# ReLU-squared attention and a gated MLP on one core: queries split earlier, weights decoded earlier, TensorE fed zeros at the start, casts ahead of halves

## The chip, the cores and the metric

One core of a Trainium2 chip runs the whole program. The metric is the time on the device of one execution, in microseconds (us). The engines of the core work side by side, each through its own instructions in order: TensorE (PE: matmuls, with the weight loads PEld beside them), VectorE (DVE), ScalarE (ACT), GpSimd (POOL), and SyncE (SP), which here issues every DMA. TensorE reads from the on-chip memory SBUF and writes only to the accumulators in PSUM, of which the kernel uses eight tiles of 128 x 512 floats.

## The reference

```python
# u, v: (4, 3008, 256)   z: (4, 3008, 64)   w_gate, w_val: (256, 1536)   w_out: (1536, 256)
scores = (1.0 / S) * np.matmul(z, z.transpose(0, 2, 1))
attn = np.maximum(scores, 0.0) ** 2
x = (u * np.matmul(attn, v)).reshape(B * S, D)
rms = np.sqrt(np.mean(x * x, axis=-1, keepdims=True) + 1e-06)
xn = x / rms * rms_g
g = xn @ w_gate
silu = g * (1.0 / (1.0 + np.exp(-g)))
out = (silu * (xn @ w_val) @ w_out).astype(np.float32)
```

Inputs arrive as float32 (z, u, v) and, for the weights, as 64-bit floats, which the kernel takes apart into 32-bit words itself.

## The kernel before

**Precision.** TensorE multiplies in a short float format (float32r). Every operand is therefore split into a high half (a cast) and a low half (operand minus high half), and a product is three matmuls: high by high, low by high, high by low. Keys have 64 dimensions only, so their high and low half stand in the two halves of the 128 partitions, and a score product is two matmuls. The cast is mostly ScalarE's work and the subtraction VectorE's; for the batches after the first, and for the weights, GpSimd does subtractions in pieces of 128 columns (L133, L348).

**Tiling.** A batch of 3008 rows is cut into six column groups of at most 512 queries, two to a pair, so there are 12 pairs, three in a batch. For each pair p there are two phases. Phase ("A", p) is the attention: 24 steps, one for each tile of 128 keys, the last tile having 64. Phase ("M", p) is the norm and the MLP: 12 units, one for each 128 columns of the hidden layer, with three slots each, so slots 0 to 35. The MLP's two input products are done as one 2 x 2 block product with seven products in place of eight (Winograd's form); A11, A12, S1, S2, S3, A22, S4 name the seven operands of x, in the order in which a unit takes them. The order of phases is A0, A1, A2, M0, A3, M1, A4, M2 and so on: the attention runs three pairs ahead.

**A step of an attention phase** (`phase_a`). Step i issues the score product of step i+2 (`emit_s`: high and low half of the queries, tiles mh0, ml0, mh1, ml1, against a key tile in zst; ScalarE's ReLU; VectorE's multiplication ReLU times score, L416), then the halves of step i+1 (`emit_l`: H by ScalarE's cast, L438, and L by VectorE's subtraction, L441), then the jobs hooked on step i, then the product of step i with v (`emit_av`, L482, L483, L487: six matmuls for each of two column groups). For the tile of 64 keys the low half is put into the other 64 partitions of H (L445), and the product is four matmuls. In some steps (`is_square`) ScalarE makes the square itself, twice (L435, L436), and VectorE's multiplication drops out. Scores are symmetric: from the second batch on, a tile whose mirror image will be needed later is also copied as two 16-bit halves (`halves`, L456 on VectorE or L458 on ScalarE) and stored; the mirror is later loaded transposed (`load_turned`), and its score product is left out. In the first batch this happens only within the third pair.

**At the end of a pair** the products with v of the last two steps are put off in a queue (`pend`): the second half of step 22, and the two halves of step 23, each of which is followed by its gate (L512: accumulator times u, read by VectorE, then stored). Between them, `enter_a` issues the next pair's first two score products. The next pair's queries are loaded into buffers of tag `raw` and split by VectorE (L290 high, L291 low, `prep_mov`) at step 22.

**Around the phases.** During the first three attention phases, which have 72 steps counted through, the weights are decoded: a part is a load, one square on ScalarE, five VectorE operations (L154, L160, L166, L170, L174) and sums on GpSimd; then the seven combinations of each of three groups of weights are made, split and stored to DRAM (L133, L224, L229), and in each MoE unit loaded again (wu). The norm of a pair (squares, sums, a root by a cubic and two Newton steps in small operations L563 to L584, scaling) and the split of its x (L642 high, L647 low) are hooked on steps of a later attention phase or are placed by a planner (`Beside`) on slots of an MLP phase: it gives VectorE 0.75 us of room in each slot and ScalarE 1.35 in each third one, and puts each job in the first slot with room. The planner also places the next batch's key and value casts (`plan_batch`), each a given number of slots after its load.

**The start** loads the first keys and v, splits them and begins; the first pair's queries come from the same load as the first keys.

Of the kernel before, what the change touches and what calls it, by code (L numbers as in the profile page):

```python
# [19 lines left out]
P = 128  # L20
CH = 512
# [9 lines left out]
def kernel(  # L31
# [84 lines left out]
    def prep_const():  # L116
        nc.vector.memset(warm, 0.0)

        nc.scalar.activation(warm, warm, AF.Silu)
        nc.sync.dma_start(out=g_sb, in_=gT)  # L120
        nc.sync.dma_start(out=fold_sb, in_=fold)
# [152 lines left out]
    def prep_mov(p, k):  # L274
# [12 lines left out]
        def split():  # L287
            mh = moving.tile([P, CH], F32R, tag=f"mh{k}", name="mh")
            ml = moving.tile([P, CH], F32R, tag=f"ml{k}", name="ml")
            nc.vector.tensor_scalar(mh[:, :n], tiles["raw"][:, :n], SCALE, None, op0=ALU.mult)  # L290
# [5 lines left out]
        return load, split, tiles  # L296
# [87 lines left out]
    def is_square(p, i, k):  # L384
        return p < LAG and (i + k) % 2 == 1 and not is_turned(p, i, k) and (p < LAG - 1 or i < NK - 8)
# [40 lines left out]
    def emit_l(p, i, ks=(0, 1)):  # L426
        b, c0 = where(p)[:2]
        kt = order(p)[i]
        for k in ks:
# [16 lines left out]
            att[p, i, k] = (hi, lo)  # L446
            kc = kt // 4
            if kc > c and keeps(b, c, kc):
# [6 lines left out]
                if c0 == 0 and copies[0] % 5 in (1, 3):  # L455
# [454 lines left out]
    def plan_splits(p, phase, slots):  # L910
        jobs_ = split_jobs_at(p)
        if p == 0:
            jobs_ = [jobs_[i] for i in (2, 3, 6, 5, 4, 0, 1)]
# [9 lines left out]
    def plan_batch(b):  # L923
# [4 lines left out]
        for k, (load, one, two) in enumerate(todo):  # L928
            if k == NC and b == 1:
                m.put(norm_plan(1)[:13], 3)  # L930
# [5 lines left out]
            h = m.put([("a", 0.6, 0, one), ("d", 0.7 if dve else 0.0, 0, two)], s + 2)  # L936
# [17 lines left out]
    plan_splits(0, ("A", 2), [16, 17, 18, 19, 20, 21, 22])  # L954
    at(("A", 2), NK - 1, lambda: load_x(1))
    for p in range(1, NPAIR):
# [6 lines left out]
        if p == 1:  # L963
            for i, (e, cost, gap, fn) in enumerate(norm_plan(1)[13:]):
# [20 lines left out]
    for p in range(1, NPAIR):  # L985

        for k in range(2):
            load, split, _ = prep_mov(p, k)
# [4 lines left out]
            else:  # L993
                at(("A", p - 1), NK - (5 if p == 1 else 10), load)
                at(("A", p - 1), NK - 2, split)
# [32 lines left out]
    for j, steps, end in ((0, (5, 9, 13, 17), 26), (1, (24, 28, 32, 36), 39), (2, (40, 44, 48, 51), 54)):  # L1028
# [6 lines left out]
    for f, g in zip(range(0, 8, 2), (54, 58, 62, 66)):  # L1035
        plan_part(prep_wout(f), g)

    with tc.manual_schedule():
# [6 lines left out]
        for c in range(2):  # L1045
            first["z", c][1]()
            first["m", c][1]()
            first["z", c][2]()
            if c == 0:
                first["v", 0][1]()  # L1050
                first["v", 0][2]()
        emit_s(0, 0)
        first["v", 1][1]()
        emit_s(0, 1)
        first["v", 1][2]()
        emit_l(0, 0)
        for p in range(LAG):
            phase_a(p)
            if p + 1 < LAG:
                for go in enter_a(p + 1):  # L1060
                    go()
                    pend.popleft()()
# [46 lines left out]
```

## Time and profile before

| | |
|---|---|
| median of 3 runs | 2063.69 us (2063.58 to 2065.18) |
| the profiled execution | 2068.19 us, span 2066.4 us |
| TensorE busy | 2028.0 us, 98% of the span, 8968 matmuls |
| VectorE busy | 1598.0 us, 77% |
| ScalarE busy | 1448.5 us, 70% |
| GpSimd busy | 217.3 us, 11% |
| DMA | 320.50 MB, 155 GB/s |

The span runs from the first to the last instruction of the profile. A busy time is the union of an engine's instructions; a matmul's own duration (387 to 389 ns on the mean) overlaps with the next, so one comes about every 0.22 us. The releaser of a wait is the instruction that ended it. PEclk is the clock granted to TensorE as a share of 2.4 GHz.

### The profile page before, as it was taken

What the parts mean: (1) busy time and instruction counts of PE and PEld (TensorE: products, weight loads), DVE (VectorE), ACT (ScalarE), POOL (GpSimd) and SP (SyncE); (2) the same over time, 40 slices, a digit from 0 to 9 for tenths busy, and PEclk for the clock granted to TensorE, in tenths of its full rate; (3) what the DMA queues carried; (4) which work ended last, traced back from release to release, by engine and by line L of the source; (5) the groups of instructions that cost most, each with busy time, mean ns of one, the idle gap of its engine ahead of it and who ended that gap; (6) DMA issues with size and microseconds to landing.
All of it is one profiled execution on the core that took longest, in us unless ns stands there. A gap on an engine that the chain in (4) does not pass through costs nothing.

```text
span 2066.4 us, 27204 instructions
## 1 busy us (share of the span) xinstructions
PE 2028.0 (98%) x8968; PEld 1679.2 (81%) x8968; DVE 1598.0 (77%) x2633; ACT 1448.5 (70%) x2601; POOL 217.3 (11%) x376
## 2 busy tenths in 40 slices
PE   8998999999999999999999999999999999999999
PEld 7787778788888888888887888788888788888887
DVE  7788988997867778787775876878777677777765
ACT  8887867785686666697577675679657757466665
POOL 0155845100000000400000000220000000000000
PEclk9999999999999999999999999999999999999999
DMA  3245375254555496337365458634545637734342
GB/s 109 67 129 166 104 251 191 89 189 169 138 153 191 125 211 203 130 142 226 114 165 168 148 140 196 218 110 164 197 128 132 210 134 159 198 119 161 124 145 91
DMA packets 320654, 320.50 MB, mean 155 GB/s; under 512 B 196736, under 2 KB 235776, under 8 KB 320512
## 3 DMA queue, kind: packets, MB, share of 16 engines
q1 hardware_dynamic: 320512, 318.77, 50.8%
q8 instruction: 70, 1.15, 0.2%
q14 instruction: 72, 0.59, 0.1%
HBM read 190.78 MB, written 81.79 MB: 132 GB/s over the span
## 4 chain that ended last, share of the span: by engine, by line
PE 76%; DVE 2%; ACT 2%; DMA 1%; issue 1%; SPq 0%; ACTq 0%; DVEq 0%
PE ps L681 10%; PE ps L682 9%; PE ps L683 9%; PE po L482 9%; PE po L483 9%; PE po L487 8%; PE py L709 5%; PE py L713 5%; PE py L710 5%; PE ps L402 3%; PE ps L401 3%; DMA raw<-in_zT 1%; ACT s L688 1%; ACT hH L693 1%; DMA out_T<-y 0%
## 5 line engine op out<-in xcount | busy, mean ns | idle before, releaser
L482 PE MATMUL po<-H,vh 128*128 128x512 f32 (+1 forms) x1152 | 448.7, 389 | 7.7 <-DVE H L445 5.1
L483 PE MATMUL po<-H,vl 128*128 128x512 f32 (+1 forms) x1152 | 445.8, 387 | 0.0
L688 ACT COPY s<-ps 128x512 f32<-128x512 f32 (+1 forms) x432 | 250.0, 579 | 221.8 <-PE ps L683 221.8
L681 PE MATMUL ps<-xh,wu 128*128 128x512 f32 (+1 forms) x1008 | 392.4, 389 | 7.4 <-ACT s L688 4.9
L683 PE MATMUL ps<-xl,wu 128*128 128x512 f32 (+1 forms) x1008 | 389.1, 386 | 2.9 <-DVE xl L647 2.9
L682 PE MATMUL ps<-xh,wu 128*128 128x512 f32 (+1 forms) x1008 | 389.2, 386 | 0.4 <-DMA wu<-wc 0.2
L487 PE MATMUL po<-L,vh 128*128 128x512 f32 (+1 forms) x1104 | 337.9, 387 | 4.4 <-DVE L L441 4.2
L693 ACT CAST hH<-s 128x512 fp32r<-128x512 f32 (+1 forms) x288 | 177.0, 615 | 200.3 <-DVE s L775 197.1
L441 DVE TENSOR_TENSOR L<-r,H 128x512 fp32r<-128x512 f32 x368 | 254.7, 705 | 50.7 <-ACT H L438 29.0
L416 DVE TENSOR_TENSOR r<-ps,r 128x512 f32<-128x512 f32 x328 | 214.4, 680 | 98.3 <-ACT r L409 97.7
L409 ACT ACTIVATE r<-ps 128x512 f32<-128x512 f32 (+1 forms) x392 | 215.7, 597 | 105.8 <-PE ps L402 95.1
L698 DVE TENSOR_TENSOR hL<-s,hH 128x512 fp32r<-128x512 f32 (+1 forms) x288 | 199.6, 693 | 107.4 <-ACT hH L693 94.2
L482 PEld LDWEIGHTS po<-H,vh 128*128 128x128 f32 x1152 | 216.8, 188 | 58.3 <-DVE H L445 11.2
L483 PEld LDWEIGHTS po<-H,vl 128*128 128x128 f32 x1152 | 217.1, 188 | 40.1
L487 PEld LDWEIGHTS po<-L,vh 128*128 128x128 f32 x1104 | 206.9, 188 | 48.1 <-DVE L L441 9.5
L681 PEld LDWEIGHTS ps<-xh,wu 128*128 128x128 f32 x1008 | 189.3, 188 | 53.0 <-ACT s L688 12.9
L709 PE MATMUL py<-hH,woh 128*128 128x512 f32 (+1 forms) x576 | 222.5, 386 | 0.1
L710 PE MATMUL py<-hH,wol 128*128 128x512 f32 (+1 forms) x576 | 222.1, 386 | 0.0
L683 PEld LDWEIGHTS ps<-xl,wu 128*128 128x128 f32 x1008 | 189.3, 188 | 39.6 <-DVE xl L647 3.6
L682 PEld LDWEIGHTS ps<-xh,wu 128*128 128x128 f32 x1008 | 189.4, 188 | 35.7 <-DMA wu<-wc 1.2
L438 ACT CAST H<-r 128x512 fp32r<-128x512 f32 x328 | 202.2, 626 | 1.9 <-DVE r L416 1.9
L348 POOL TENSOR_TENSOR vl<-raw,vh 128x128 fp32r<-128x128 f32 x144 | 78.9, 584 | 981.8 <-ACT vh L337 981.8
(82 smaller groups left out, 2915.4 us busy)
## 6 DMA issues: line engine op xcount, KB each, us to landing
wu<-wc SPq DMA_DIRECT2D x288, 448.0 KB, 4.0
kept<-halves SPq DMA_DIRECT2D x168, 256.0 KB, 2.0
raw<-in_v SPq DMA_DIRECT2D x44, 256.0 KB, 4.1
u<-in_uT SPq DMA_DIRECT2D x40, 256.0 KB, 4.5
xg<-u SPq DMA_DIRECT2D x40, 256.0 KB, 2.1
raw<-in_zT SPq DMA_DIRECT2D x38, 256.0 KB, 4.5
ux<-xg SPq DMA_DIRECT2D x16, 512.0 KB, 4.8
out_T<-y SPq DMA_DIRECT2D x32, 256.0 KB, 2.2
```

What stands on the lines that cost most here:

```text
L409: nc.scalar.activation(a[:, :n], ps[:, :n], AF.Relu)
L416: nc.vector.tensor_tensor(a[:, :n], ps[:, :n], a[:, :n], op=ALU.mult)
L441: nc.vector.tensor_tensor(lo[:, :n], a[:, :n], f32(hi[:, :n]), op=ALU.subtract)
L482: nc.tensor.matmul(po[d][:, :n], wh[:, j, ds], hi[:, :n], start=(i == 0), stop=False)
L483: nc.tensor.matmul(po[d][:, :n], wl[:, j, ds], hi[:, :n], start=False, stop=(ends and lo is None))
L487: nc.tensor.matmul(po[d][:, :n], wh[:, j, ds], lo[:, :n], start=False, stop=ends)
L681: nc.tensor.matmul(ps[:, :n], wh[:, o, :], xh[:, :n], start=start, stop=False, skip_group_check=True)
L682: nc.tensor.matmul(ps[:, :n], wl[:, o, :], xh[:, :n], start=False, stop=False, skip_group_check=True)
L683: nc.tensor.matmul(ps[:, :n], wh[:, o, :], xl[:, :n], start=False, stop=stop, skip_group_check=True)
L688: nc.scalar.copy(s, ps[:, :self.n])
L709: nc.tensor.matmul(acc[h, d][:, :n], woh[:, f, ds], hi[:, :n], start=(f == 0), stop=False)
L710: nc.tensor.matmul(acc[h, d][:, :n], wol[:, f, ds], hi[:, :n], start=False, stop=False)
```

## The change

- `prep_const`: a tile of zeros (tag H, 512 columns) is written by VectorE, and TensorE multiplies it by itself eight times.
- The split of the queries gets two callable halves. At the start the order is: first keys' cast, query high, keys' low, query low, second query's split, v's cast, first score product; the second keys' cast and low half come after the first `emit_l`.
- `is_square`: for the first two pairs steps 22 and 23 are squared no more on ScalarE; for the third pair squares reach to step 21 instead of 15.
- `emit_l`: both casts and subtractions of a step come ahead of both copies into halves. The copies of the middle pairs of a batch (c0 = 2), too, go to VectorE two times in five.
- The x splits of the first pair run in the order of use, and one step earlier.
- `plan_batch`: eight instead of thirteen operations of the second pair's norm lie in M0; the others run in A3. The first two casts of a batch's keys start four slots after their loads, not two.
- Queries of the second and third pair: the first is split at step 21, the second at step 22.
- Decode parts, combinations and w_out parts begin earlier (of 72 steps): the parts at 4, 8, 12, 16, then 21, 25, 29, 33, then 37, 40, 43, 47; the combinations at 20, 36, 50; w_out at 50, 55, 59, 63.
- At a change of pair the put-off products go ahead of the next pair's score products, one for one.

```diff
+        idle = moving.tile([P, CH], F32R, tag="H", name="idle", bufs=5)
+        nc.vector.memset(f32(idle), 0.0)
+        none = ps_s.tile([P, CH], F32, tag="ps", name="ps")
+        for _ in range(8):
+            nc.tensor.matmul(none, idle[:, :P], idle, start=True, stop=True)
...
-        return p < LAG and (i + k) % 2 == 1 and not is_turned(p, i, k) and (p < LAG - 1 or i < NK - 8)
+        return p < LAG and (i + k) % 2 == 1 and not is_turned(p, i, k) and i < NK - 2
...
             att[p, i, k] = (hi, lo)
+            made_[k] = a
+        for k, a in made_.items():
+            c = c0 + k
+            n = width(c)
             kc = kt // 4
...
-                if c0 == 0 and copies[0] % 5 in (1, 3):
+                if c0 <= 2 and copies[0] % 5 in (1, 3):
...
-        if p == 0:
-            jobs_ = [jobs_[i] for i in (2, 3, 6, 5, 4, 0, 1)]
...
-                m.put(norm_plan(1)[:13], 3)
+                m.put(norm_plan(1)[:8], 3)
...
-            h = m.put([("a", 0.6, 0, one), ("d", 0.7 if dve else 0.0, 0, two)], s + 2)
+            h = m.put([("a", 0.6, 0, one), ("d", 0.7 if dve else 0.0, 0, two)], s + (4 if k < 2 else 2))
...
-    plan_splits(0, ("A", 2), [16, 17, 18, 19, 20, 21, 22])
+    plan_splits(0, ("A", 2), range(15, 15 + NO))
...
-            for i, (e, cost, gap, fn) in enumerate(norm_plan(1)[13:]):
+            for i, (e, cost, gap, fn) in enumerate(norm_plan(1)[8:]):
...
-                at(("A", p - 1), NK - 2, split)
+                at(("A", p - 1), NK - 3 + k, split)
...
-    for j, steps, end in ((0, (5, 9, 13, 17), 26), (1, (24, 28, 32, 36), 39), (2, (40, 44, 48, 51), 54)):
+    for j, steps, end in ((0, (4, 8, 12, 16), 20), (1, (21, 25, 29, 33), 36), (2, (37, 40, 43, 47), 50)):
...
-    for f, g in zip(range(0, 8, 2), (54, 58, 62, 66)):
+    for f, g in zip(range(0, 8, 2), (50, 55, 59, 63)):
...
-        for c in range(2):
-            first["z", c][1]()
-            first["m", c][1]()
-            first["z", c][2]()
-            if c == 0:
-                first["v", 0][1]()
-                first["v", 0][2]()
+        first["z", 0][1]()
+        first["m", 0][3]()
+        first["z", 0][2]()
+        first["m", 0][4]()
+        first["m", 1][1]()
+        first["v", 0][1]()
         emit_s(0, 0)
+        first["v", 0][2]()
         first["v", 1][1]()
         emit_s(0, 1)
+        emit_l(0, 0)
         first["v", 1][2]()
-        emit_l(0, 0)
+        first["z", 1][1]()
+        first["z", 1][2]()
...
                 for go in enter_a(p + 1):
+                    pend.popleft()()
                     go()
-                    pend.popleft()()
```

## Rows read from the trace of the kernel before

**Rows 1.** The page: busy us, share, instructions of each engine; engines' shares of the chain

```profile
PE 2028.0 (98%) x8968; PEld 1679.2 (81%) x8968; DVE 1598.0 (77%) x2633; ACT 1448.5 (70%) x2601; POOL 217.3 (11%) x376
...
PE 76%; DVE 2%; ACT 2%; DMA 1%; issue 1%; SPq 0%; ACTq 0%; DVEq 0%
```

**Rows 2.** TensorE's waits, whole span: total us, times, longest us

```profile
PE po L482 <- DVE H L445: 5.1, 7, 1.5
PE ps L681 <- ACT s L688: 4.9, 12, 1.9
...
PE po L487 <- DVE L L441: 4.2, 7, 1.0
PE ps L683 <- DVE xl L647: 2.9, 1, 2.9
PE ps L681 <- DVE s L775: 2.5, 1, 2.5
```

**Rows 3.** Windows: busy us (and count) by engine, granted clock, DMA share, GB/s

```profile
0.00:10.00 10.00, 4.30 (x10) 2.84 (x11) 4.97 (x9) 5.63 (x10) 0.20 (x4) 1.00 0.76 236
...
80.00:100.00 20.00, 18.37 (x72) 14.13 (x71) 13.73 (x23) 12.77 (x24) 4.50 (x8) 0.91 0.29 93
100.00:120.00 20.00, 18.89 (x83) 15.20 (x83) 15.50 (x26) 16.07 (x30) 3.69 (x8) 1.00 0.42 146
120.00:140.00 20.00, 20.00 (x90) 16.57 (x89) 17.90 (x28) 18.63 (x36) 12.46 (x20) 1.00 0.41 119
...
180.00:200.00 20.00, 15.55 (x55) 11.31 (x54) 14.40 (x23) 12.69 (x24) 13.58 (x24) 0.83 0.47 140
```

**Rows 4.** Windows by phase: third, first MoE block, first, second attention phase

```profile
198.00:280.50 82.50, 77.44 (x342) 63.24 (x343) 79.33 (x119) 68.39 (x130) 59.62 (x88) 1.00 0.50 147
280.50:380.00 99.50, 93.43 (x406) 75.05 (x404) 81.36 (x131) 66.36 (x122) 39.19 (x69) 1.00 0.58 192
10.50:92.00 81.50, 80.97 (x355) 66.29 (x354) 65.35 (x105) 72.30 (x134) 8.94 (x20) 1.00 0.21 65
93.00:184.50 91.50, 88.59 (x378) 71.50 (x378) 76.14 (x125) 76.17 (x141) 48.65 (x83) 0.98 0.42 127
```

**Rows 5.** Groups by line and shape: count, busy us, mean ns, idle before

```profile
L441 DVE TENSOR_TENSOR L<-r,H 128x512 fp32r<-128x512 f32 x340 | 235.2, 701 | 45.1 <-ACT H L438 26.0 <-ACT r L436 18.1
...
L458 ACT COPY halves<-r 128x1024 uint16<-128x1024 uint16 x126 | 134.6, 1068 | 5.5 <-DMA kept<-halves 4.1 <-DVE L L441 1.4
...
L456 DVE COPY halves<-r 128x1024 uint16<-128x1024 uint16 x42 | 28.8, 687 | 0.0
```

**Rows 6.** Timeline at the first change of pair: start, us, instruction, idle before

```profile
91.57 1.29 DVE L445 TENSOR_TENSOR H<-r,H 64x512 fp32r<-64x512 f32 x2 [0.49 <-ACT r L436]
...
93.37 0.49 PE L401 MATMUL ps<-mh,zst 128*128 128x512 f32 x1 [1.32 <-DVE mh L290]
...
103.14 0.47 PE L482 MATMUL po<-H,vh 128*128 128x512 f32 x1 [1.11 <-DVE u L512]
```

**Rows 7.** Timeline at the second change of pair

```profile
185.21 1.80 DVE L441 TENSOR_TENSOR L<-r,H 128x512 fp32r<-128x512 f32 x2
...
187.66 0.80 PE L401 MATMUL ps<-mh,zst 128*128 128x512 f32 x1 [3.34 <-DVE mh L290]
```

**Rows 8.** Timeline near the end of the first MoE block

```profile
369.37 0.38 DVE L584 SCALAR_TENSOR_TENSOR misc<-misc 128x32 f32<-128x32 f32 x1
```

**Rows 9.** Timeline in the MoE block of the seventh pair

```profile
1296.73 0.62 ACT L313 CAST zst<-raw 128x512 fp32r<-128x512 f32 x1 [3.88 <-DMA raw<-in_zT]
...
1298.40 0.50 PE L681 MATMUL ps<-xh,wu 128*128 128x512 f32 x1 [1.88 <-ACT s L688]
```

**Rows 10.** Window after that wait, TensorE alone: busy us (count), clock, DMA share, GB/s

```profile
1300.00:1320.00 20.00, 20.00 (x84) 0.93 0.62 203
```

**Rows 11.** Timeline at the fifth pair's tile of 64 keys

```profile
622.22 0.50 PE L482 MATMUL po<-H,vh 128*128 128x512 f32 x1 [0.77 <-DVE H L445]
```

**Rows 12.** Timeline at the second pair's tile of 64 keys

```profile
173.59 0.50 PE L482 MATMUL po<-H,vh 128*128 128x512 f32 x1 [0.93 <-DVE H L445]
```

More of the change, by code (lines that the diff above doesn't have):

```diff
@@ L285, in load, with high, low @@
             nc.sync.dma_start(out=raw[:, :n], in_=zT2[:, t0 + k * CH:t0 + k * CH + n])
-        def split():
-            mh = moving.tile([P, CH], F32R, tag=f"mh{k}", name="mh")
+        def high():
+            mh = tiles["mh"] = moving.tile([P, CH], F32R, tag=f"mh{k}", name="mh")
+            nc.vector.tensor_scalar(mh[:, :n], tiles["raw"][:, :n], SCALE, None, op0=ALU.mult)
+        def low():
+            mh = tiles["mh"]
             ml = moving.tile([P, CH], F32R, tag=f"ml{k}", name="ml")
-            nc.vector.tensor_scalar(mh[:, :n], tiles["raw"][:, :n], SCALE, None, op0=ALU.mult)
             nc.vector.scalar_tensor_tensor(
@@ L294, in split @@
             mov[p, k] = (mh, ml)
-        return load, split, tiles
+        def split():
+            high()
+            low()
+        return load, split, tiles, high, low
     def prep_stat(b, c, shared=None):
@@ L428, in emit_l @@
         kt = order(p)[i]
+        made_ = {}
         for k in ks:
@@ L987 @@
         for k in range(2):
-            load, split, _ = prep_mov(p, k)
+            load, split = prep_mov(p, k)[:2]
             if p >= LAG:
```

## The prediction, made before the change was run

> **What bounds the kernel now.** I read the page's busy shares and its chain first: the reader sees TensorE busy 98% of the span and holding 76% of the chain that ends last [rows 1]. No other engine can be the bound of the whole, so all a change of order can win is the time in which TensorE stands still or is clocked down. The profiled execution took 2068.19 us around a span of 2066.4; 2066.4 less 2028.0 busy is 38.4 us of standing still. The second view says on whom TensorE waits: the five rows of [rows 2] alone add up to 19.6 us. The third, the windows by time, says where. An undisturbed window has 90 matmuls in 20 us, 0.222 us each; the first 200 us hold the large holes [rows 3]. After that the losses are single waits, which the timeline places.
>
> I cut the losses into seven places, and price the change at each.
>
> **1. Start.** TensorE is busy 4.30 of the first 10 us, idle 5.70 until the first keys are split, and its first ten matmuls take 0.43 each [rows 3]. The change lets it multiply zeros meanwhile: one memset of 512 columns on VectorE, eight matmuls of about 0.43, 3.4 us in all, over before 5.7 if the memset ends before 2.2. It also puts the key's low half ahead of the query's, one operation of 0.7 (nearest row 0.701, [rows 5]) out of the way of the first product, and moves the second key cast and its subtraction behind the first weights. No row shows such a memset or the zeros; bounds: -0.5 us (the zeros run late and the keys wait) and +2.8 (0.7 plus ten matmuls at 0.222 instead of 0.43, 2.1). Since ScalarE and VectorE, not TensorE, feed the first products, I take the small end: 0.7.
> The row shows slow first matmuls after an idle start, although the granted clock reads 1.00 there [rows 3]. The Trainium skill (TensorE: Matmul & The Clock Gate, "Part 1: The HAM clock gate") says that the throttled state is the default and that activity releases it; by that rule the zeros would bring the full 2.1. Nothing below needs this.
>
> **2. First pair to second (80 to 104 us).** Lost now: 1.63 us idle and 0.09 of 20 us of clock, 1.8, in the first window, and 1.11 in the next, 4.5 in all [rows 3]. Before, both queries are split behind the last tile's two subtractions on VectorE (91.57 to 92.86), and TensorE, out of work, waits 1.32 us for the first (till 93.37) [rows 6]. After, the first query's two operations (0.5, from 92.86 to 93.37, and one like the 0.701 of [rows 5]; 1.2) go ahead of these, and one more six-matmul group (1.33 us) stands before the product. So the first query's half comes in time. The second query still queues behind the two subtractions, and VectorE carries more: two multiplications that ScalarE's squares did (2 x 0.701, 1.4), the first query's 1.2 and the first two operations of a decode part (at most 1.4; I take 1.0). Against this stand the idle shares: VectorE is busy 65.35 of 81.50 us in this phase [rows 4], 0.7 us free in a step of 16 matmuls (3.6 us), 2.1 over three steps. The subtractions then end near 92.86 + 1.4 + 1.2 + 1.0 - 2.1 = 94.4, the second query's halves at 94.9 and 95.6; TensorE arrives at 93.37 - 1.32 + 1.33 + 0.44 = 93.8. About 1.5 us of idle is left, as now. The gates (awaited 1.11 us until 103.14 [rows 6]) are split: the first column's comes early, the second's still stands behind four operations; I leave 0.8 of that wait. Half the clock loss may go, 0.9. Gain 0.1 + 0.3 + 0.9 = 1.3, between 0 and 4.5.
>
> **3. Second pair to third (180 to 200 us).** Lost now: 4.45 idle and 0.17 of 20 us of clock, 3.4: 7.85 [rows 3]. Here VectorE is late: its last two subtractions run 185.21 to 187.01, and TensorE waits 3.34 us until 187.66 [rows 7]. The same reordering gives 1.33 us of cover and takes the first query from behind them, but two multiplications (1.4) and the last operation of a part (0.7) come in ahead of the second query, and no idle time on VectorE is there to take them. Cover and price nearly cancel; I take 1.0 for a shorter slow stretch, between -1.5 and 7.
>
> **4. Third pair and its way into the MoE (198 to 285 us).** VectorE is busy 79.33 of 82.50 us [rows 4]: it is the bound of this phase, and TensorE's standing still is 5.06 us there. At its end TensorE waits 2.89 us for the low half of x [rows 2], since the splits of x were run in another order, the half needed first last. The change takes from VectorE here 1.4 decode parts (five operations each, 7 x 0.701 = 4.9 as an upper price; I take 4, as masks are shorter) and five multiplications (squares reach to step 21 instead of 15), 3.5: 7.5 us less. That is more than 5.06. It also runs the x splits one step earlier and in the order of use, so the 2.89 goes. ScalarE gains five passes like the cast of 0.62 in [rows 9], 3 us, and is busy 68.39 of 82.50, so it covers them, though not in steps 16 to 19 where I leave 1. And about 1.3 of the 5.06 is the wait for gates before 200 us, counted in place 3 (as the 1.11 of [rows 6], with a small second one). Gain 5.06 + 2.89 - 1 - 1.3 = 5.6; ends 1 and 7.9.
>
> **5. End of the first MoE block.** TensorE waits 2.5 us for VectorE [rows 2], which has just run the small operations of the norm's root, the last of them 0.38 us at 369.37 [rows 8]. Those thirteen move into the fourth pair's phase. The query split stays behind. What is late next is that split, 1.1 us for one query, which the slack of a MoE step took before. Two casts land in the block's last slot instead of one (0.6). Gain 2.4; ends 1 and 2.5.
>
> **6. Loads of the next batch's keys (MoE blocks of the fourth and seventh pair).** ScalarE, in order, stands 3.88 us at a cast for a load of z, and TensorE behind it 1.88 [rows 9]; the earlier twin is in the same row of [rows 2] (4.9 us, 12 times, most of the others 0.2). 4.9 - 1.88 - 10 x 0.2 leaves about 1.0 for it. The change starts the first two casts two slots later, that is in the next unit, about 7.5 us (99.5 us for 12 units [rows 4], with a little off for waits). The load is then long in. A slow stretch behind the second wait costs 0.07 of 20 us, 1.4 [rows 10]. The casts bunch later: where the block is full their buffers are the queries' own, and those would wait for POOL; by slots one unit apart, that fits. Gain 1.9 + 1.0 + 1.4 = 4.3; ends 2.5 and 4.6.
>
> **7. Halves in the middle pair of batches 2 to 4.** In the fifth pair TensorE waits 0.77 us at the last key tile for VectorE's subtraction [rows 11], for ScalarE's copies of halves (1.068 us, [rows 5]) stand between its casts. Seven such waits make 5.1 us [rows 2]; less 0.93 in the second pair [rows 12], which has no halves, 4.2. The change puts both casts ahead of both copies and hands two copies in five to VectorE (0.687), some eight a pair: ScalarE loses 8.5 us, VectorE gains 5.5. Gain 2.9, ends 1.5 and 4.2.
>
> **Sum.** 0.7 + 1.3 + 1.0 + 5.6 + 2.4 + 4.3 + 2.9 = 18.2 against 2068.2, so 2050.0 for an execution like the profiled one. The median of the three runs, 2063.69, lies 4.5 lower. Waits that come from the order are in every execution, slow stretches perhaps not; 15.0 of the sum hold without those of places 2, 3 and 6 (0.9 + 0.9 + 1.4). I take the whole off the median all the same, since what place 3 holds is priced low: **2045.5**.
>
> **Rivals.**
> *A: the two pair changes come back too.* If VectorE's free time suffices, places 2 and 3 give 4.5 + 7.85 instead of 2.3, 10 more: 2035.5. For it: the extra six matmuls and the earlier first query; against: the second query is behind the same subtractions, and VectorE has no gap before 187 [rows 7].
> *B: the third pair stays VectorE's.* GpSimd's pieces move with the decode, and VectorE's subtraction takes 0.701 us on the mean, but 0.90 as one of the two in 1.80, while GpSimd is at work [rows 5, 7]. If the pieces now fall on subtractions that ran alone, 38 of the 48 of a phase at 0.2 us use up the 7.5 us, place 4 gives 1 for 5.6, and places 2 and 3 nothing: 18.2 - 4.6 - 2.3 = 11.3, so 2052.4. The Trainium skill (SBUF — State Buffer, "Who interferes with whom") says that a VectorE operation with two inputs in SBUF and a GpSimd operation exclude each other, one waiting whole; the rows agree in sign, and this rule speaks against the change.
> *C: slower.* VectorE takes on in the first two phases one part and a bit (4), four multiplications (2.8) and dearer operations (3), 9.8 us, and its idle time (16.2 and 15.4 us [rows 4]) can't be used because it lies elsewhere in the steps. Then 9.8 goes on the path at the pair changes, with a clock drop at each that lasts as long as the worst now (2 x 3.4): 16.6 lost. With nothing from places 2 to 4, the rest gives 0.7 + 2.4 + 4.3 + 2.9 = 10.3, so 2070. It decides from 10.3 us of loss on; against it, the first phase has a fifth of VectorE free.
> *D: the reordering does nothing* (each wait is replaced by one as long): places 1 to 5 at nought and 6 and 7 as forecast, 7.2: 2056.5.
>
> **Chances.** Forecast 0.57 (2040 to 2050), A 0.18, B 0.15, D 0.06, C 0.04. The low end takes in most of A, 2035; the high end B and half of what lies to D, 2055. A measurement of this kernel tells 0.2%, some 4 us, from no change: faster 0.95, same 0.02, slower 0.03.
>
> **What would show it.** In the profile after: PE busy about 2028 plus the eight zeros, span some 20 us less. Place 1: matmuls before the first keys. 2 and 3: a remaining wait of the query product on mh of the second query, of 1 to 3 us; if it is gone, A. 4: the wait for xl gone, VectorE's busy share from 198 us on clearly under 96%; if it stays, B. 5: no wait on L775's successor near 370. 6: no wait of a z cast on its load. 7: fewer and shorter waits on the 64-partition subtraction. New waits on mh of the second query over 4 us, or on buffers of x in the third pair, would make the forecast wrong.

## The result: 2046.55 us, and the profile after

The changed kernel took 2046.55 us (median of 4 runs, 2046.25 to 2047.41) where the kernel before took 2064.43 beside it (4 runs, 2063.58 to 2065.52): a ratio of 0.9914, 95% interval 0.9897 to 0.9931. Forecast were 2045.5 us and, as a difference of medians, 18.2 us; it is 17.9. The profiled execution took 2047.41 us, span 2045.6, and so lies 20.8 us below the profiled one of before.

The page of the changed kernel: busy us, share and instructions by engine, and the shares of the chain.

```profile
PE 2023.9 (99%) x8976; PEld 1680.8 (82%) x8976; DVE 1610.9 (79%) x2657; ACT 1426.3 (70%) x2578; POOL 225.8 (11%) x376
...
PE 88%; DVE 4%; ACT 3%; issue 2%; POOL 2%; DMA 1%; SPq 0%; DVEq 0%; ACTq 0%; POOLq 0%
```

Eight more matmuls, and yet less busy time: the mean granted clock is 0.998 for 0.996. 21.7 us of standing still are left of 38.4 [rows 1]. TensorE's waits over the whole span (total us, times, longest us), answering [rows 2]:

```profile
PE ps L415 <- DVE mh L296: 4.4, 3, 2.1
PE po L506 <- DVE L L456: 3.0, 4, 1.3
PE po L501 <- DVE u L531: 2.1, 2, 1.6
PE ps L700 <- ACT s L707: 1.8, 11, 0.2
PE ps L124 <- DVE idle L121: 1.5, 1, 1.5
...
PE po L501 <- DVE H L460: 0.8, 1, 0.8
```

The waits for xl (2.9) and for the norm's root (2.5) are gone, those for the 64-key tile fell from 5.1 to 0.8, ScalarE's s from 4.9 to 1.8. What is left is at the two pair changes. The windows that answer [rows 3] and, last, the third pair of [rows 4] up to its own first product of the MoE:

```profile
0.00:10.00 10.00, 7.21 (x20) 4.68 (x20) 4.67 (x9) 5.38 (x10) 0.20 (x4) 1.00 0.57 168
80.00:100.00 20.00, 17.51 (x70) 13.81 (x69) 18.07 (x28) 12.51 (x25) 14.79 (x24) 0.92 0.47 142
100.00:120.00 20.00, 19.85 (x87) 15.94 (x86) 16.77 (x26) 17.45 (x34) 9.38 (x15) 0.99 0.57 187
...
180.00:200.00 20.00, 13.43 (x51) 9.46 (x52) 15.97 (x27) 11.62 (x21) 8.80 (x14) 0.98 0.61 172
200.00:220.00 20.00, 19.79 (x86) 16.81 (x86) 17.73 (x28) 16.91 (x33) 13.02 (x20) 0.93 0.48 151
198.00:276.04 78.04, 76.51 (x338) 64.23 (x339) 74.70 (x110) 68.04 (x129) 57.84 (x84) 0.98 0.52 156
```

From 180 to 200 us TensorE did even less than before (51 matmuls for 55); from 80 to 100 GpSimd is busy 14.79 us for 4.50. In the third pair VectorE has 3.3 us free where it had 3.2, but the stretch is 4.5 us shorter. It is busy 74.70 of 78.04 us there, 95.7%, so the prediction's sign, a share clearly under 96%, did not show, although the time fell.

To place gain and loss I took the same matmuls in both traces and the time between them: the first change (from the key product that starts at 86.02 us in the changed kernel to the one at 104.77), the second change (177.77 to 209.19), the third pair from there to the first product of the MoE (276.04), and the first MoE block up to the first key product behind it (366.65).

| place | forecast gain | gain by the traces |
|---|---|---|
| 1 start (up to the second step, 14.36 to 13.43) | 0.7 | 0.9 |
| 2 first change, 19.13 to 18.75 | 1.3 | 0.4 |
| 3 second change, 29.34 to 31.42 | 1.0 | -2.1 |
| 4 third pair, 72.00 to 66.85, and the wait for xl, 2.9 | 5.6 | 8.0 |
| 5 end of the first MoE block, wait for the root | 2.4 | 2.5 |
| 6 MoE blocks of the fourth (91.46 to 90.29) and seventh pair (93.32 to 90.30) | 4.3 | 4.2 |
| 7 middle pairs of batches 2 to 4 (78.68, 78.64, 79.40 to 77.57, 77.59, 77.61) | 2.9 | 4.0 |
| not priced: last pairs of batches 2 to 4, 1.2; the rest of the first MoE block (98.13 to 90.61 in all), 2.1; the remainder -0.4 | 0 | 2.9 |
| sum | 18.2 | 20.8 |

### The profile page after: what moved, and what is told of

Same layout as the page of the kernel before. It is cut to its first block, busy times and chain, and to the rows that moved or that the text cites. A ratio compares the mean times of both kernels' runs of the same rounds, so it can differ in the third digit from the quotient of the medians.

```text
span 2045.6 us, 27209 instructions
## 1 busy us (share of the span) xinstructions
PE 2023.9 (99%) x8976; PEld 1680.8 (82%) x8976; DVE 1610.9 (79%) x2657; ACT 1426.3 (70%) x2578; POOL 225.8 (11%) x376
## 4 chain that ended last, share of the span: by engine, by line
PE 88%; DVE 4%; ACT 3%; issue 2%; POOL 2%; DMA 1%; SPq 0%; DVEq 0%; ACTq 0%; POOLq 0%
PE po L501 11%; PE po L502 11%; PE po L506 11%; PE ps L700 10%; PE ps L701 10%; PE ps L702 10%; PE py L728 6%; PE py L729 6%; PE py L732 6%; PE ps L416 4%; PE ps L415 4%; POOL w L140 1%; POOL wolo L140 1%; ACT s L707 1%; ACT r L423 1%
## 5 line engine op out<-in xcount | busy, mean ns | idle before, releaser
L430 DVE TENSOR_TENSOR r<-ps,r 128x512 f32<-128x512 f32 (+1 forms) x327 | 213.9, 681 | 99.7 <-ACT r L423 98.7
L456 DVE TENSOR_TENSOR L<-r,H 128x512 fp32r<-128x512 f32 x368 | 248.0, 706 | 14.4 <-ACT r L451 14.3
L453 ACT CAST H<-r 128x512 fp32r<-128x512 f32 (+1 forms) x327 | 191.5, 622 | 3.3 <-DVE r L430 3.2
```

Source lines behind the costliest of these rows:

```text
L430: nc.vector.tensor_tensor(a[:, :n], ps[:, :n], a[:, :n], op=ALU.mult)
L456: nc.vector.tensor_tensor(lo[:, :n], a[:, :n], f32(hi[:, :n]), op=ALU.subtract)
```

## The experiments

Each is the changed kernel with the edit shown. "1st", "2nd", "third", "MoE" are the four stretches in us, from one profiled execution each. Where an edit does not touch a stretch, the first change lies between 18.5 and 19.0, the second mostly between 31.4 and 31.9 (once, in z, 30.0), the third pair between 66.9 and 67.5: what is inside that is not read. The kernel before took 2064.9 to 2068.6 us (medians) beside them, so times are compared by the ratio.

| kernel | us | ratio, 95% | 1st | 2nd | third | MoE |
|---|---|---|---|---|---|---|
| before | 2064.43 | 1 | 19.13 | 29.34 | 72.00 | 98.13 |
| changed | 2046.55 | 0.9914 (0.9897, 0.9931) | 18.75 | 31.42 | 66.85 | 90.61 |
| x_casts_back | 2051.20 | 0.9924 (0.9911, 0.9936) | 18.62 | 31.86 | 68.04 | 91.13 |
| y_norm_share_back | 2054.07 | 0.9942 (0.9928, 0.9956) | 18.54 | 31.59 | 67.50 | 90.81 |
| z_zeros_xorder_back | 2048.14 | 0.9912 (0.9898, 0.9925) | 18.83 | 30.03 | 66.87 | 90.94 |
| d_decode_back | 2050.76 | 0.9923 (0.9911, 0.9935) | 15.71 | 27.64 | 71.90 | 95.74 |
| q_both_queries | 2050.04 | 0.9920 (0.9905, 0.9934) | 18.59 | 32.20 | 67.53 | 90.65 |
| u_other_buffers | 2047.51 | 0.9907 (0.9890, 0.9923) | 18.99 | 29.66 | 67.27 | 90.91 |
| o_last_av_late | 2049.74 | 0.9918 (0.9903, 0.9933) | 20.90 | 30.67 | 67.48 | 91.02 |
| s_squares_to_end | 2048.64 | 0.9911 (0.9896, 0.9926) | 19.42 | 30.13 | 66.88 | 91.60 |
| e_combine_later | 2046.47 | 0.9909 (0.9895, 0.9922) | 16.48 | 31.39 | 66.89 | 90.74 |
| g_clear_changes | 2050.36 | 0.9926 (0.9914, 0.9939) | 18.96 | 27.71 | 70.57 | 91.66 |
| h_clear_wout_in_m0 | 2057.06 | 0.9965 (0.9953, 0.9977) | 17.23 | 27.80 | 68.86 | 100.60 |
| f_gap_and_u | 2046.10 | 0.9892 (0.9876, 0.9909) | 15.19 | 30.75 | 66.85 | 90.98 |

**x_casts_back.**

```
- s + (4 if k < 2 else 2)
+ s + 2            # and the copies of halves again within the loop over the two columns
```

> The changed kernel with two parts undone: the first two casts of the next batch's keys start two slots earlier again, and the casts of a step are no longer put ahead of its copies of halves (the share of the copies that VectorE makes stays widened). Theory (places 6 and 7 of the prediction by their own mechanisms): the waits of casts on their loads come back in the MoE blocks of the fourth and seventh pair, 1.2 + 3.0 = 4.2 us by the stage times of the two traces, and the pairs with halves lose some 2 us more because the second cast stands behind a copy of 1.07 us: 2047 + 6 = 2053. Rival (in the pairs with halves the widened share alone does it, the order nothing): 2047 + 4.2 = 2051. Rival (the wait for the load only moved): no change, 2047.

ScalarE's waits for the loads of z came back, 3.0 and 2.3 us in the two blocks (3.3 and 3.9 before), but TensorE paid only 0.8 and 0.2 (blocks of 91.08 and 90.47). In the seventh pair's block the load landed 4.9 us after the issue of its group began, where the one of [rows 9] took 6.45. So the delay removes the wait, as forecast; that its cost hangs on the landing I take from these two traces alone, and about 3 of the 4.2 us stay unproven. The middle pairs kept 77.6 each: there the order does nothing, the rival was right. It is worth 0.8, 0.8 and 0.3 in the last pairs of batches 2 to 4, and perhaps 1 in the third pair, which copies halves too.

**y_norm_share_back.**

```
- norm_plan(1)[:8]  ... [8:]  ; c0 <= 2 and copies[0] % 5 in (1, 3)
+ norm_plan(1)[:13] ... [13:] ; c0 == 0 and copies[0] % 5 in (1, 3)
```

> The changed kernel with two other parts undone: thirteen instead of eight operations of the norm stand in the first MoE block again, and VectorE makes its share of the copies of halves in the first pair of a batch only. Theory (places 5 and 7): the first MoE block loses 2.5 us, the fourth pair gets 0.6 back, the middle pairs of batches 2 to 4 lose about 2.4 of the 3.95 that they gained: 2047 + 4.3 = 2051. Rival (in the middle pairs the order alone does it): 2047 + 1.9 = 2049. Rival (the first block's gain of 7.5 is that of the splits of x alone): the block's time is unchanged.

The root comes back, but in another place than the theory had it: as 1.9 us of the fourth pair (85.07 to 87.01; 84.41 in the kernel before) and 0.2 of the block before; TensorE waits 1.2 us at 370.64, behind the root's small operations on VectorE. The middle pairs lose 1.0, 0.9 and 3.5. The third of these is a wait and its echo; the timeline of TensorE in that pair (start, us, instruction, idle before it):

```profile
1611.09 0.50 PE L501 MATMUL po<-H,vh 128*128 128x512 f32 x1 [2.01 <-DVE H L460]
...
1612.13 0.56 PE L501 MATMUL po<-H,vh 128*128 128x512 f32 x1
1612.49 0.63 PE L502 MATMUL po<-H,vl 128*128 128x512 f32 x1
...
1615.05 0.63 PE L502 MATMUL po<-H,vl 128*128 128x512 f32 x1
1615.47 0.46 PE L501 MATMUL po<-H,vh 128*128 128x512 f32 x1
1615.77 0.39 PE L502 MATMUL po<-H,vl 128*128 128x512 f32 x1
```

Behind 2.01 us of standing still eight matmuls (1612.13 to 1615.47) come 0.42 us apart on the mean instead of 0.23, another 1.5 us. So place 7 is VectorE's share of the copies: about 1 us in each of two middle pairs, and 3.5 in the third, nearly all of it this wait and its echo, which one execution shows. Place 5 was worth 2.1, forecast 2.4.

**z_zeros_xorder_back.**

```
- eight matmuls of zeros and their memset
+ if p == 0: jobs_ = [jobs_[i] for i in (2, 3, 6, 5, 4, 0, 1)]
```

> The changed kernel without the zeros at the start, and with the splits of the first x in the old order. Theory: the zeros are worth 0.2 to 0.4 us at the first product of weights and values, and the x order 2.9 us at the start of the first MoE block: 2047 + 3.2 = 2050. Rival (the zeros bring the clock up for the first ten matmuls): another 2 us, 2052. Rival (the first MoE block's 7.5 us came from elsewhere, the freed VectorE): the wait for the low half of x doesn't come back, 2047.5.

The wait for xl did not come back, the block took 0.3 us more: the rival was right, the order of the splits was not what TensorE waited for. The second step begins at 13.84 us without the zeros and at 13.43 with them in the changed kernel, but the other kernels, whose starts are not edited and have the zeros, fall into two groups. In x, y, d, q, e and h, as in the changed kernel, the key products behind the first two start 0.23 us apart, and the second step begins at 12.98 to 13.47. In u, o, s, g and f most of them start 0.43 us apart, as here without the zeros, and it begins at 13.96 to 14.22; in s and g the granted clock reads 0.50 from 7.85 to 11.2 us. So the zeros came with the higher clock (2.4 GHz) for the first key products in seven of twelve executions, and were worth 0.4 to 0.9 us there; in the other five they were worth nothing. What decides it, no run shows. Nowhere did they bring the 2.1 us that the prediction had worked out for the higher clock: where the products are fast, TensorE next stands still for ScalarE's first cast, 0.82 us until 10.58 in the changed kernel.

**d_decode_back.**

```
- (0, (4, 8, 12, 16), 20), (1, (21, 25, 29, 33), 36), (2, (37, 40, 43, 47), 50) ; w_out (50, 55, 59, 63)
+ (0, (5, 9, 13, 17), 26), (1, (24, 28, 32, 36), 39), (2, (40, 44, 48, 51), 54) ; w_out (54, 58, 62, 66)
# and the splits of x from step 16 on in the old order
```

> The changed kernel with the old, later steps for the decode of the weights, their combination and the output weights, and the splits of the first x one step later in the old order. Theory (place 4): the third pair has VectorE as its bound again and loses 4 us, the start of the first MoE block 2.9 or more, the two pair changes gain some 1 us by less work of GpSimd and VectorE before them: 2047 + 6 = 2053. Rival B of the prediction (the load only moved, VectorE's subtractions just run dearer elsewhere): nothing beyond the x order, 2050.

This run settled most. The third pair takes 71.90 us, as before, and the wait for xl is back (2.0 us, with the clock at 0.83 over the next ten): the early decode gives 5.1 + 5.1 us there (the splits' order and their start, one step later here, are in this edit too; the start was not tried by itself). But the changes fall to 15.71 and 27.64: it costs 3.0 + 3.8 at them. The timeline of VectorE at the first change shows why, first with the old steps, then in the changed kernel:

```profile
89.92 0.41 DVE L296 TENSOR_SCALAR mh<-raw 128x512 fp32r<-128x512 f32 x1
90.44 0.69 DVE L301 SCALAR_TENSOR_TENSOR ml<-raw,mh 128x512 fp32r<-128x512 f32 x1
91.16 1.29 DVE L460 TENSOR_TENSOR H<-r,H 64x512 fp32r<-64x512 f32 x2
92.49 0.43 DVE L296 TENSOR_SCALAR mh<-raw 128x512 fp32r<-128x512 f32 x1
```

```profile
89.71 0.69 DVE L296 TENSOR_SCALAR mh<-raw 128x512 fp32r<-128x512 f32 x1
90.50 0.77 DVE L301 SCALAR_TENSOR_TENSOR ml<-raw,mh 128x512 fp32r<-128x512 f32 x1
91.19 0.68 DVE L161 TENSOR_SCALAR wt<-wraw 128x512 uint32<-128x512 uint32 x1
91.97 0.76 DVE L167 SCALAR_TENSOR_TENSOR wraw<-wraw,wt 128x512 uint32<-128x512 uint32 x1
92.77 1.70 DVE L460 TENSOR_TENSOR H<-r,H 64x512 fp32r<-64x512 f32 x2
94.49 0.57 DVE L296 TENSOR_SCALAR mh<-raw 128x512 fp32r<-128x512 f32 x1
```

Two decode operations stand ahead, and all of them are dearer: GpSimd is at work from 89.38 to 100 in the second, not at all in the first. The second query comes 2.0 us later, 1.7 of it beyond the 0.3 by which the run with the old steps was ahead. TensorE, in the changed kernel:

```profile
95.11 0.50 PE L415 MATMUL ps<-mh,zst 128*128 128x512 f32 x1 [2.13 <-DVE mh L296]
95.97 0.50 PE L416 MATMUL ps<-ml,zst 128*128 128x512 f32 x1 [0.36 <-DVE ml L301]
```

With the old steps these two waits are 0.29 and 0.23, and the clock stays at 1.00.

**q_both_queries.**

```
- at(("A", p - 1), NK - 3 + k, split)
+ at(("A", p - 1), NK - 3, split)
```

> The changed kernel with the second query of the next pair split at the same step as the first, ahead of the last tile's two subtractions. Theory: what TensorE waits for at the two pair changes is the second query behind those subtractions, so its waits of 2.13 and 1.65 us for it go, with the slow stretch behind the first: 2 to 4 us less, 2044. Rival (VectorE as a whole is late there, and the subtractions are then awaited in its place): the sum of the waits at a change stays, 2047, with the product of weights and values waiting 1 to 2 us more.

The rival, nearly to the letter: the waits for mh are gone, and TensorE waits 1.7 us for the 64-key tile's subtractions and 1.9 for what follows. The clock does not fall at the first change (granted 1.00 for 0.91), but TensorE stands still 3.5 us for 2.6. The first change takes 18.59, the second 32.20.

**u_other_buffers.**

```
- (("u", 1), ("raw", 2), ("raw", 2), ("out", 3))[2 * k + d] ; NK - 3: (0, 0) ; NK - 1: the other three
+ (("u", 1), ("out", 3), ("raw", 2), ("raw", 2))[2 * k + d] ; NK - 3: (0, 0), (0, 1) ; NK - 1: the other two
```

> The changed kernel with the gates' u pieces in other buffers (the first column's second piece in one of the three that halves use, the last piece in one of the raw buffers), and the first column's two pieces loaded at once, three steps before the end of a pair. Theory: at the second pair change VectorE stands 3.72 us at the second gate operation for a load whose buffer the query split frees; with the load early this goes, TensorE's 1.61 and 0.4 us behind it too: 2 us less, 2045, and VectorE's late share of work in the third pair falls by as much. Rival (VectorE is late there anyhow): VectorE's wait goes, TensorE's stays as a wait for the next operation, 2047.

In the changed kernel VectorE, with its gates now ready earlier, stands here:

```profile
192.06 0.68 DVE L531 TENSOR_TENSOR u<-po,u 128x512 f32<-128x512 f32 x1
196.46 0.69 DVE L531 TENSOR_TENSOR u<-po,u 128x512 f32<-128x512 f32 x1 [3.72 <-DMA u<-in_uT]
```

The theory had the place right and the reason wrong. SP issued this load at 193.18, but the split of the second query had ended at 190.13 and left its buffer free. What held the load is what stands ahead of it among SP's DMAs, the store of a combined weight that GpSimd had not finished; GpSimd's last pieces, SP's wait for them (window 184 to 196) and SP's queue in the changed kernel:

```profile
190.35 2.35 POOL L140 TENSOR_TENSOR wolo<-w,wohi 128x128 fp32r<-128x128 f32 x4
```

```profile
SPq L236 <- POOL wolo L140: 6.5, 1, 6.5
```

```profile
192.72 0.36 SPq L236 DMA_DIRECT2D wc<-wolo  x1
193.18 1.43 SPq L521 DMA_DIRECT2D u<-in_uT  x3
```

In the kernel before, the gates came at 198.02 and the load, issued at 189.27, was there. The other buffers help because they let the second piece be loaded ahead of that store; the later pieces still stand behind it (store at 193.59, load at 194.06), and 0.9 us of the wait moved to one of them. The second change takes 29.66, 1.8 less, but not all of that is the edit's: z, with the old buffers, took 30.03, and TensorE stands still 5.25 us there and 5.26 here. In both, the clock had fallen by 191.6 us (granted 0.50), so that TensorE was slow while VectorE waited; in the changed kernel it fell only behind the wait, at 199.3. Like with like, the edit is worth some 0.4 us, or 0.7 by f, which has it too and where the clock fell at 198.7. The ratio, 0.9907, does not tell it from the changed kernel.

**o_last_av_late.**

```
- pend.popleft()(); go()
+ go(); pend.popleft()()
```

> The changed kernel with the old order at the two pair changes: the first scores of the next pair stand ahead of a six-matmul group of the last pair's weights and values. Theory (place 2): the group is 1.33 us of cover for the query, so TensorE waits that much more at each of the two changes: 2047 + 2.7 = 2050. Rival (VectorE is as late in either order, and the group only moves the wait): 2047.

At the first change the wait for mh grows to 3.3 us and the change to 20.90: the cover is worth 2.1 there. At the second, 30.67, no loss shows: TensorE waits 2.02 us for mh instead of 1.65, but comes so late to the products behind the gates that it does not wait for these.

**s_squares_to_end.**

```
- ... and i < NK - 2
+ ... and i < (NK - 2 if p == LAG - 1 else NK)
```

> The changed kernel with the squares of the last two steps of the first two pairs on ScalarE again (two multiplications less on VectorE ahead of each of these pair changes). Theory: VectorE is 1.4 us sooner at the change and ScalarE has the room: each change gains up to 1.4, 2045. Rival (ScalarE's casts for the last subtractions are late by as much): 2047; if ScalarE is the one that is full there: 2049.

Mixed: 19.42 at the first change (the wait for mh grew to 2.5), where the two multiplications were not what made VectorE late. At the second, 30.13, they were a part of it: there TensorE waits for two subtractions in the changed kernel,

```profile
181.06 0.73 PE L506 MATMUL po<-L,vh 128*128 128x512 f32 x2 [1.32 <-DVE L L456]
185.19 0.74 PE L506 MATMUL po<-L,vh 128*128 128x512 f32 x2 [1.10 <-DVE L L456]
```

and with the edit these waits are 0.48 and 0.62. The first MoE block takes 1.0 more, of which 0.9 is a wait for weights (wu), and the ratio is the same.

**e_combine_later.**

```
- end of the first group: 20, 21, 22, 23, 25, 27, 28, 30, 32
+ 26, 26, 27, 27, 28, 29, 30, 31, 32
```

> The changed kernel with one thing moved: the combination of the first decoded weights (GpSimd's pieces) begins at step 26 instead of 20, behind the first pair change; the decode's own operations on VectorE stay where they are, two of them ahead of the second query. Theory (GpSimd makes VectorE dear at the change): with GpSimd idle the last two subtractions take 1.29 us instead of 1.70 and the second query's two operations 1.1 instead of 1.4, the multiplication and the operations before them 0.3 less; TensorE's wait for the second query falls from 2.13 to about 1.2 us and the slow stretch behind it goes (1.8 us), as with the decode put back: the first change gains 2 to 3 us, 2047 - 2.5 = 2044.5. Rival (the two decode operations of 1.44 us are the cause): the wait falls by 0.5 us at most, the clock falls again, 2046.5. Rival (the pieces come to lie on the next steps and cost there what they save here): 2047.

The decode's operations stay, GpSimd is gone from 83 to 96 us, and the first change falls by 2.3. The lines that answer those above:

```profile
90.59 0.42 DVE L161 TENSOR_SCALAR wt<-wraw 128x512 uint32<-128x512 uint32 x1
91.11 0.69 DVE L167 SCALAR_TENSOR_TENSOR wraw<-wraw,wt 128x512 uint32<-128x512 uint32 x1
91.83 1.29 DVE L460 TENSOR_TENSOR H<-r,H 64x512 fp32r<-64x512 f32 x2
93.16 0.43 DVE L296 TENSOR_SCALAR mh<-raw 128x512 fp32r<-128x512 f32 x1
```

TensorE waits 0.91 us for the second query and the clock does not fall (granted 1.00 over the change for 0.91): of the 2.3 us, 0.7 are standing still, from 2.6 to 2.0, and 1.6 the slow stretch. Some 1.4 us came back in the second pair, where ScalarE stood 2.19 us at a cast for GpSimd's now denser pieces. So of the 3.0 us that the decode costs at the first change, 2.3 go with the first combination. That it is GpSimd's pieces beside VectorE, and not the combination's casts on ScalarE that moved with them, rests on the lines above: the same operations of VectorE are back at their undisturbed times.

**g_clear_changes, h_clear_wout_in_m0.**

```
+ (0, (4, 7, 10, 13), (15, 16, 17, 17, 18, 19, 20, 25, 26)), (1, (25, 28, 31, 34), (36, ..., 42, 50, 51)),
+ (2, (37, 40, 43, 49), (52, 53, 54, 55, 57, 59, 60, 62, 64)) ; w_out (52, 56, 60, 64) ; u as in u_other_buffers
# and the splits of the first x in the old order
# h: w_out (53, 57, 61), and the fourth decode of w_out in the first MoE block, loaded at its slot 3
```

> The changed kernel with both pair changes kept free of the decode: the first weights' parts a little closer together and their combination from step 15 on, interrupted in steps 21 to 24; the second weights' parts from 25 on, their combination from 36 to 42 and from 50; the last part behind the second change; the output weights one to two steps later; the first x split in the old order; the gates' u pieces in the other buffers and loaded early. Theory: the first change falls to the 15.7 us that it took with the decode put back (3.0 less), the second to 27.6 (3.8 less); the third pair gets back one part of the decode (3.4 us of VectorE) and loses 1 to 3; sum -4, 2043. Rival (the decode needs the time that the changes had, and VectorE is late in the third pair and at the splits of x, as with the old steps): 2047 to 2050.

> As the one before, with one of the four decodes of output weights in the third pair moved into the first MoE block (6.5 us of VectorE less in the third pair than with four). Theory: the third pair stays at the 66.9 us of the changed kernel, the MoE block has the room (VectorE 84% busy there): 2047 - 6.8 = 2040. Rival (VectorE of the MoE block is full in its first third, or the load of these weights takes the DMA queues from the expert weights): the block's 90.6 us become 92 to 94, 2043.

In both the second change falls by 3.6 to 3.7 us, as forecast. The first does not in g: GpSimd, with its pieces closer together, was still at them until 95 us. In h, with the same steps there, it takes 17.23, because the clock did not fall (granted 1.00 for 0.91). The third pair pays 3.7 for the part that it got back. In h it pays 2.0, but the MoE block loses ten. TensorE waits 4.34 and 1.82 us for its weights (wu), with the granted clock at 0.50 from 340.2 to 346.9 us, and the DMA queues are not the cause. SP's queue, the longest waits of SP in it (window 318 to 342), and the window from 324 us on (columns as above):

```profile
320.90 15.61 SPq L343 DMA_DIRECT2D raw<-in_v  x3
336.61 0.88 SPq L684 DMA_DIRECT2D wu<-wc  x2
```

```profile
SPq L343 <- DVE zst L331: 19.0, 3, 13.0
```

```profile
324.00:334.00 10.00, 9.83 (x43) 7.58 (x42) 9.52 (x13) 7.35 (x15) 10.00 (x16) 1.00 0.07 24
```

SP stands 15.61 us over three loads of v, at a DMA share of 0.07, and the weights are issued behind them. GpSimd is busy the whole window, but what ends SP's wait of 13.0 us is VectorE: the next batch's key subtractions, which free these buffers. The lines of VectorE:

```profile
318.94 0.69 DVE L331 TENSOR_TENSOR zst<-raw,zst 64x512 fp32r<-64x512 f32 x1
333.49 0.84 DVE L331 TENSOR_TENSOR zst<-raw,zst 64x512 fp32r<-64x512 f32 x1
```

The block's six key subtractions begin 28 to 61 us behind its first product, in the changed kernel 18 to 44. As I read the code, the planner takes the added decode's operations off the room that it gives VectorE, and so puts the key subtractions into later slots. The first half of the rival comes nearest: VectorE has no room where the decode was put, and the block pays for it through SP's queue.

**f_gap_and_u.**

```
+ (0, (4, 8, 12, 16), (15, 15, 16, 26, 27, 29, 30, 32, 34)), (1, (24, 27, 30, 33), 36), the third group as it was
+ u as in u_other_buffers
```

> The changed kernel with the first change kept free of the decode and the second freed of its load: the first weights' combination is cut in two (its first three steps at 15 and 16, the rest from 26 on), the second weights' parts start at step 24 instead of 21, and the gates' u pieces have the other buffers and are loaded early. The third pair's work is as in the changed kernel. Theory: the first change falls from 18.75 us to 15.7 to 16.5 (no piece of GpSimd and no decode operation ahead of the second query), the second from 31.4 to 29.7, the third pair and the first MoE block stay at 66.9 and 90.6: 2047 - 4 = 2043, a ratio to the kernel before of 0.990. Rival (what the changes save comes back as late VectorE or ScalarE in the second pair, as two waits on ScalarE of 0.5 and 0.7 us did when the whole combination started at 26): 2046, 0.991.

The first change takes 15.19, the best of all, GpSimd idle from 87 to 105; TensorE's only wait for a query's half there is 0.23. The second is 30.75: the third u piece, issued at 192.01 behind the store at 191.54, now ends VectorE's wait of 1.86. About 0.9 us were lost on a subtraction at 78 us and 0.7 in the second pair. The ratio of 0.9892 (0.9876 to 0.9909) is the lowest, but its interval overlaps with the changed kernel's; the profiled times differ by 1.3 us. That it is faster is likely and not shown.

## Why the prediction was right, and where its steps were wrong

The time came out within 1.1 us, and a part of that is luck. By the traces the seven places sum to 17.9 us for the 18.2 forecast, because places 2 and 3 fell short by 4.0 and places 4 and 7 gave 3.5 more. Places that I had not priced gave another 2.9. Against this, I had worked out the sum on an execution of 2068.19 us and took it off a median of 2063.69, and the two traces lie 20.8 us apart, the medians 17.9: the 2.9 us between cancel the 2.9 that were not priced. In which places they lie no run shows, since there is one trace of the kernel before.

- Place 1: 0.7 forecast, 0.9 by the traces. This is partly chance: in five of the twelve executions with zeros the second step began at 13.96 us or later. Without the zeros (z) the new order of the first splits takes it from 14.36 to 13.84, so the order gave 0.5, if one execution each can tell.
- Place 2: 1.3 forecast, 0.4. The step that failed is the time of the second query's halves. I took VectorE's added operations at their undisturbed price against 2.1 us of idle time and got 94.9 for its high half. It came at 95.06, and the kernel was 0.9 us ahead by then: 1.0 us later than worked out. The idle time was there only without GpSimd, whose pieces I had priced, in rival B, for the third pair; here I had put nothing for them. And I had the clock recover by half: it fell again (0.91 over 18 us, in both).
- Place 3: 1.0 forecast, with -1.5 as lower end; -2.1. The step that failed is "cover and price nearly cancel". The cover held: the wait for the query fell from 3.34 to 1.65 us. The price was too small. TensorE now waits 1.32 and 1.10 us for subtractions in the steps ahead of the change, where it did not before. With the decode put back one wait of 0.51 is left of these (d), and with the two multiplications given back they are 0.48 and 0.62 (s): both have a share. The other missing term is the gate's u, whose load I had not looked at; it stood in SP's queue behind a store of GpSimd's pieces, VectorE waited 3.72 us for it and TensorE 1.61. With the decode out of the way (d, g, h) the change takes 27.6 to 27.8.
- Place 4: 5.6 forecast, 8.0. VectorE's relief gave the whole 5.15 us, not 5.06 less deductions of 2.3 (e and f, with other work ahead of the pair, have the same 66.9). The wait for xl went, but not for the reason given: with the old order of the splits and the new decode it stays away (z), with the old decode, and the splits a step later, it is back (d). VectorE was late, not the order wrong.
- Place 5: 2.4 forecast; 2.5 went, 2.1 came back when undone. The fourth pair, which took over the operations, became 0.7 longer (84.41 to 85.07).
- Place 6: 4.3 forecast, 4.2 between the two traces; undone, only 1.0 of it came back, with a load that landed sooner.
- Place 7: 2.9 forecast, 4.0, and 5.4 when undone, most of it in one wait of one execution. I had named both the order and the share; it is the share. The order of casts gives 1.2 to 1.9 in the last pairs, which I had not priced.

Of the rivals, B had the right mechanism and put its price in the wrong place: GpSimd's pieces beside VectorE's operations cost 2.3 us, with the clock's fall behind them, at the first change, and the third pair gained all the same. Of A's prize 3.9 of the 4.5 us were to be had at the first change (f) and 1.7 of the 7.85 at the second (d), but not with the decode where the change puts it. C's waits came, without its size.

## What to carry to other kernels

When work is moved off the bound stretch, look at what runs at the hand-over where it lands: here 10 us gained in one phase cost 7 at two changes of pair, and GpSimd's share of that was in no instruction of the critical engine. When an operation is made earlier, check each of its inputs, loads above all: whose buffer they wait for, and what stands ahead of them in the queue that issues them. A wait removed by putting one operation ahead of another on a full engine only changes its name; ask first whether the engine as a whole is late.

## What the runs showed of the hardware

- GpSimd beside VectorE: with it at work the subtraction pair of the 64-key tile takes 1.70 us for 1.29, the queries' multiplication 0.57 to 0.69 for 0.42, and four pieces of GpSimd 3.24 for 1.72 (w<-w,w) and 2.83 for 1.47 (w<-wraw). The multiplication ReLU times score, one of whose inputs is in PSUM, keeps its 0.68 beside them. The Trainium skill (SBUF — State Buffer, "Who interferes with whom") has it that a VectorE operation with at most one input in SBUF, outside the two-port modes, does not contend with GpSimd, and that one with two does when GpSimd reads SBUF; by that rule the trace agrees for the subtractions and for the multiplication ReLU times score. The queries' multiplication has one input in SBUF and was lengthened all the same; whether it ran in a two-port mode no run shows. The Trainium skill also says there that the loser blocks for the whole instruction; no operation of VectorE was lengthened by more than 0.35 us in any of these traces, and one piece of GpSimd with VectorE out of its way takes 0.40 to 0.46.
- TensorE's clock after a stand-still: it fell to the lower level (1.2 GHz) behind waits of 2.01 us (y) and 2.13 us (the changed kernel), each time at a cost of some 1.5 us; behind 1.7 us it stayed at 1.00 in two kernels (h and q), behind 1.8 us (g) and in the kernel before behind 1.32 us (0.91) it fell. The length of one wait alone does not decide it.
- A DMA that has to wait in SP's queue held those behind it, in both places where this was looked at: a store that waited 6.5 us for GpSimd held the loads of u, and a load that waited 13.0 us for VectorE held the weights, at a DMA share of 0.07.
- The first load of a group for the next batch's keys had landed 4.9 us after the group's issue began in one execution and 6.4 in another. The TensorE time lost behind them was 0.2 and 3.0 us; that the landing makes this difference is likely, and no run isolates it.
